# GpSimd's small steps in order of their inputs, three norms of one unit on VectorE, and the filter's turns and weight loads ordered otherwise around it

## The chip, the cores and the metric

The kernel runs on one core of one Trainium2 chip. The metric is the device time of one execution in microseconds (us). All times below are in us unless ns is said.

A core's engines each work off their own instruction stream, and wait for each other at semaphores: TensorE (PE; PEld is its weight load), VectorE (DVE), ScalarE (ACT), GpSimd (POOL) and SyncE (SP), which here only issues DMAs. A DMA that SyncE or GpSimd issues stands in that engine's queue (SPq, POOLq), and runs beside the engines.

## The reference, cut to what matters

Two layers, each a gated long convolution and a GeGLU MLP, over S = 2048 tokens of D = 576 channels, with a hidden size F = 4608. Both layers use the same weights and the same k, v.

```python
def A(q, k, v, shift_k, ssm_k, ssm_D):          # q is the normed x
    k_shift = sum over t < 4 of k_pad[:, t:t+S] * shift_k[:, 3-t]
    kv = k_shift * v
    y = irfft(rfft(kv, 2S) * rfft(ssm_k, 2S))[:S]  # causal convolution along the tokens
    y = y + kv * ssm_D
    return q * y

def B(x):
    return (gelu(x @ w_gate) * (x @ w_up)) @ w_down

x = A_q
x = x + A(layernorm(x), k, v, ...)
x = x + B(layernorm(x))
x = x + A(layernorm(x), k, v, ...)
x = x + B(layernorm(x))
```

The convolution's result y does not depend on x, so both layers use one y; x enters A only through the norm that gates it.

## The kernel before, in words

**Units and passes.** The 2048 tokens are four chunks of 512, a chunk is four pieces of 128 tokens. A unit is one chunk in one layer. There are eight: unit 0 is (layer 0, chunk 0), 1 is (0,1), 2 is (1,0), 3 is (1,1), 4 is (0,2), 5 is (0,3), 6 is (1,2), 7 is (1,3). The passes are [0], [1,2], [3,4], [5,6], [7]: the MLP's weights are streamed through SBUF once in each pass, and the units of a pass share them. A pass has three phases (a third of the hidden size each), and in each phase each of its units has one visit: a gate/up stage of 12 hidden tiles (L1555, `gu`; ScalarE's gelu at L1559, VectorE's product at L1560), then a down stage of four accumulations, one for each piece (L1575, `dn`), which VectorE adds into the residual `x_c` (L1611, or L1606 with the row sum where a layer ends; L1597 into a result tile `ob` where layer 1 ends). TensorE's PSUM comes as tiles of one ring with the tag "pr".

**Weights.** Gate and up weights come in groups of four hidden tiles, `load_wgu(n)`: three DMAs on SyncE (L1137 to L1139). Three such buffers exist, and nine groups make a pass, so groups 9 to 17 serve units 1 and 2, 18 to 26 units 3 and 4, 27 to 35 units 5 and 6, 36 to 44 unit 7. Down weights are `load_wd` (L1147). Loads wait in the list `due` with a due time; `weights()` issues them at once, unless a unit's input is being made (`near`) and the load is due more than HOLD = 14 later.

**The conv work between.** The convolution is done as an FFT by matmuls, and its small steps fill gaps: `conv.V` (VectorE), `conv.L` (loads and turns), `conv.Pq` (TensorE), `conv.spills` and `conv.late` (GpSimd's DMAs). The filter's `turn(b)` puts a chunk of the filter (`hb`, L419) through four DMA transposes on SyncE, and stores it to `Td` on GpSimd; `filt(b)` loads it back in another order (`hT`, L438, GpSimd), multiplies it by the FFT matrices, and spills the results to `Hd` (L399, GpSimd).

**A unit's input.** `prep(ui, j)` gates piece j on VectorE with y (`mul`, then `add`, L1224, which also sums the row). Then comes a chain of small steps, handed from engine to engine: `mean_after` (GpSimd, `nm`, L1175), `square_task` (ScalarE, `junk`, L1183), `root` (GpSimd, `ve` L1190, `rstd` L1191, `nb` L1195), `norm` (ScalarE, `xn`, L1246, two activations, one of 576 columns and one of the first 64 columns again), and `spread` (SyncE, two DMA transposes into `xnT`, L1265). The next gate/up stage multiplies `xnT`. Where layer 0 ends, a piece of a unit in layer 1 is gated with the same chain in front of it: its mean, squares and root come from the down stage's result.

**What sets the order.** The instruction order is written by a small planner at build time. It keeps an estimated clock for TensorE, VectorE and ScalarE (`t.pe`, `t.dve`, `t.act`) with fixed costs (`C_*`). Between the matmul groups it calls `fill`, which issues due weights, loads and turns, transposes of finished pieces (`spreads`), VectorE's tasks (`run_vq` from the queue `vq`, and `conv.run_v`), at most one ScalarE task (`run_aq`: first the norms in `nq`, then the squares in `aq`), and GpSimd's steps (`conv.flush`). GpSimd's small steps (the means and roots) and its DMAs stand in one queue, `spills`, first in, first out: a step goes when the one at the head is due. A small step is due AHEAD = 3.0 before its input is expected:

```python
        conv.spills.append((when - AHEAD, run))
...
    def flush(self, now, keep=0):
        while len(self.spills) > keep and self.spills[0][0] <= now:
            self.spills.popleft()[1]()
```

At run time each engine goes through its instructions in that order and waits where an input or a buffer is not there yet.

Of the kernel before, what the change touches and what calls it, by code (L numbers as in the profile page):

```python
# [16 lines left out]
ALU = mybir.AluOpType  # L17
# [16 lines left out]
C_GU, C_DN = 1.944, 0.245  # L34
C_PR = 1.25
C_BF, C_TB, C_R4 = 0.41, 0.46, 0.77
C_SQ, C_TINY, C_NA, C_ROOT, C_NB = 0.85, 0.6, 0.95, 1.5, 0.4
N_KC, N_SM, N_EO, N_HR = 4, 4, 4, 3
C_AC, C_AB = 0.76, 0.76
C_TT, C_ST, C_HT, C_GELU, C_EVA, C_EVD = 0.76, 0.82, 0.69, 0.6, 0.66, 0.76  # L40
LAG = 0.25
AHEAD, CHAINED = 3.0, 2.5
LATE = (1, 2)
HOLD, LEAD, HURRY, SPARE = 14.0, 1.8, 2.6, 4.0

# [39 lines left out]
class Conv:  # L85
# [9 lines left out]
    def __init__(self, spare, tc, ctx, pace, A_k, A_v, A_shift_k, A_ssm_k, A_ssm_D, ident, psp, cpsp, ypool):  # L95
        self.tc, self.nc, self.t = tc, tc.nc, pace
        self.spare = spare
        self.k2, self.v2, self.hk = A_k[0], A_v[0], A_ssm_k
        self.S, self.D = self.k2.shape
        self.NB = self.S // BS  # L100
        self.KS = A_shift_k.shape[1]
        self.sk, self.sD = A_shift_k, A_ssm_D
        self.ident, self.psp, self.cpsp, self.ypool = ident, psp, cpsp, ypool
        D = self.D
        pool = lambda name, bufs: ctx.enter_context(tc.tile_pool(name=name, bufs=bufs))
        self.cst = pool("c_cst", 1)
        self.krp = pool("c_kr", 3)
        self.hrp = pool("c_hr", N_HR)
        self.kcp = pool("c_kc", N_KC)
        self.ybp = pool("c_yb", 4 * RT)  # L110
        self.prp = pool("c_pr", 3)
        self.smp = pool("c_sm", N_SM)
        self.eop = pool("c_eo", N_EO)
        self.kvp = pool("c_kv", 1)
        self.Hd = [[tc.dram_tile([P, 2 * D], BF16, name=f"Hd{b}_{t}") for t in range(RT)] for b in range(self.NB)]
        self.Kd = [[tc.dram_tile([P, 2 * D], BF16, name=f"Kd{b}_{t}") for t in range(RT)] for b in range(self.NB - 1)]
        self.W = self.cst.tile([P, 24, P], BF16, name="W")
        self.Td = [None, None] + [tc.dram_tile([BS, D], BF16, name=f"Td{b}") for b in range(2, self.NB)]
        self.skc = self.cst.tile([P, self.KS, D], BF16, name="skc")
        self.y, self.yb = {}, {}  # L120
        self.kt_, self.vt_ = {}, {}
        self.y_at = {(0, j): 0.0 for j in range(RT)}
        self.kv_at, self.fwd_at, self.filt_at, self.td_at, self.hd_at = {}, {}, {}, {}, {}
        self.turn_at = 0.0
        self.y_used = {}
        self.startup, self.other = True, False
        self.h1_at = {2: 0.0}
        self.z_at, self.then = {}, []
        self.load_at, self.tight = -9.0, lambda: False
        self.nps = 0  # L130
        self.ps_free = self.spare_free = self.last = 0.0
        self.window = -1.0
        self.pr_free = [0.0] * N_SM
        self.neo, self.eo_free = 0, [0.0] * N_EO
        self.U = deque()
        self.kr_free, self.hr_free = [0.0] * 3, [0.0] * N_HR
        self.npr = self.nkr = self.nhr = 0
        self.V, self.L, self.Pq = deque(), deque(), deque()
        self.left = 0
        self.spills, self.late = deque(), deque()  # L140

    def halves(self, ap):
        return ap.rearrange("p (h c) -> p h c", h=2)
# [259 lines left out]
    def store(self, dst, t, ready):  # L403
        self.spills.append((ready, lambda: self.nc.gpsimd.dma_start(out=dst, in_=t[:])))  # L404

    def flush(self, now, keep=0):
        while len(self.spills) > keep and self.spills[0][0] <= now:
            self.spills.popleft()[1]()

    def turn(self, b):  # L410

        nc, t, D = self.nc, self.t, self.D
        own = {}

        def piece(i):
            def run():
                if i == 0:
                    own["t"] = self.kvp.tile([P, RT, D], BF16, tag="k", name="hb")
                nc.sync.dma_start_transpose(out=own["t"][:, i:i + 1, :],  # L419
                                            in_=self.hk[:, b * BS + i * P:b * BS + (i + 1) * P])  # L420
                self.turn_at = t.pe + 3.5
                if i == RT - 1:
                    def out():
                        nc.gpsimd.dma_start(out=self.Td[b].rearrange("(t p) d -> p t d", p=P), in_=own["t"][:])
                        self.td_at[b] = t.pe + 9.0
                    self.late.append((t.pe + 14.0, out))
            return run
        for i in range(RT):
            self.L.append((lambda i=i: max(self.turn_at, self.kv_at.get(1, NEVER) if b == 2 else self.td_at.get(b - 1, NEVER)),
                           piece(i)))  # L430

    def filt(self, b):
        nc, t, D = self.nc, self.t, self.D
        kc, own = {}, {}

        def load():
            own["t"] = self.kvp.tile([P, RT, D], BF16, tag="v", name="hT")
            nc.gpsimd.dma_start(out=own["t"][:], in_=self.Td[b].rearrange("(p i) d -> p i d", i=RT))  # L438
            own["at"] = t.pe + 9.0
        self.L.append((lambda: max(self.fwd_at.get(b - 1, NEVER), self.td_at.get(b, NEVER)), load))  # L440

        def out():
            if not kc:
                self.flush(NEVER)
                kc.update({k: self.kcp.tile([P, 2, D], BF16, tag="kc", name="hc") for k in range(RT)})
            return kc

        def seen(h):
            if h == 1:
                self.filt_at[b] = t.pe + 0.25  # L450

        def done(kt, h, when):
            if h == 1:
                for k in (kt, kt + 2):
                    self.spill(self.Hd[b][k], kc[k], when, (b, k))
        for h in range(2):
            self.Pq.extend(self.quarter(lambda: own["t"], out, h, lambda: max(own.get("at", NEVER), self.z_at[b - 1]()), seen, done))
            self.Pq.extend(self.then)
            self.then = []

    def step(self, m, kv=None, loaded=False):
# [65 lines left out]

        def out4():
            if not kc:
                self.flush(NEVER)  # L530
                kc.update({k: self.kcp.tile([P, 2, D], BF16, tag="kc", name="kc") for k in KTS})
            return kc

# [31 lines left out]
        def add(kt, a, part):  # L565
            def run():
                slot, pr = prs[(kt, a, part)]
                second = a == seq(kt)[1]
                if second:
                    if quad and kt % 2:  # L570
                        self.flush(NEVER)
                        f = self.kcp.tile([P, 2, HW], F32, tag="kc", name="zs")
                    else:
                        f, zslot[(kt, part)] = self.eo_tile("zs")
# [505 lines left out]
def ssm_geglu_kernel(ctx, tc, A_q, A_k, A_v, A_shift_k, A_ssm_k, A_ssm_D, B_x, B_w_gate, B_w_up,  # L1080
# [91 lines left out]
    def mean_after(v, when):  # L1172
        def run():
            v["nm"] = small.tile([P, 1], F32, tag=v["pfx"] + "nm", name="nm")
            nc.gpsimd.tensor_scalar(out=v["nm"][:], in0=v["s"][:], scalar1=-1.0 / D, scalar2=None, op0=ALU.mult)  # L1175
            v["nm_at"] = max(t.pe, when) + C_TINY
        conv.spills.append((when - AHEAD, run))

    def square_task(get_x, v):
        def run():  # L1180
# [6 lines left out]
            def root():  # L1187
# [5 lines left out]
                if "norm" in v:  # L1193
# [1 line left out]
                    nc.gpsimd.tensor_tensor(out=v["nb"][:], in0=v["nm"][:], in1=v["rstd"][:], op=ALU.mult)  # L1195
                    ready = v["rstd_at"] + C_NB
                    nq.append((lambda: NEVER if len(xn_made) >= 3 else ready, C_NA, lambda: v["norm"](ready)))
            conv.spills.append((when - AHEAD, root))
        aq.append((at_v(v, "nm_at"), C_SQ, run))

    def run_aq(limit):
        for q in (nq, aq):
            if q and q[0][0]() <= t.pe + 1.4 and max(t.act, t.pe - 1.0) + q[0][1] <= limit:
                q.popleft()[2]()
                return

    def gate2_steps(c, j, g, v, second):
        src = lambda: (x_c if second else x_b)[c][:, j, :]
# [30 lines left out]
    def prep(ui, j):  # L1239
# [2 lines left out]

        def norm(ready):
            xn = xnp.tile([P, XW], BF16, tag="xn", name="xn")
            for lo, hi, c0 in ((0, D, 0), (D, XW, 0)):
                nc.scalar.activation(out=xn[:, lo:hi], in_=x_c[c][:, j, c0:c0 + hi - lo], func=ACT.Identity,  # L1246
                                     scale=v["rstd"][:, 0:1], bias=v["nb"][:, 0:1])
            xn_made.append((ui, j, xn, t.on_act(C_NA, max(ready, t.pe - 1.0)) + 0.3))
        v["norm"] = norm
        return gate2_steps(c, j, (hvars if layer else gvars)[c][j], v, layer == 1)  # L1250

    hvars = {}

# [44 lines left out]
    def spreads():  # L1298
        while xn_made and xn_made[0][3] <= t.pe:
            ui, j, xn, _ = xn_made.popleft()  # L1300
            if j == 0:
                xnT_of[ui] = xtp.tile([P, NKC, CH], BF16, tag="xnT", name="xnT")
            spread(xnT_of[ui], j, xn)
            xn_done[ui] = j + 1

    due = []

# [4 lines left out]
    def weights():  # L1312

        while due:
            near = xn_made or nq
            if near and due[0][0] > t.pe + HOLD:
                break
            _, _, load, n = due.pop(0)
# [7 lines left out]
    def fill(limit, tensor, conv_first):  # L1326
# [3 lines left out]
        while True:  # L1330
# [3 lines left out]
            else:  # L1334
                done = run_vq(limit)
                if done is None or not (done or conv.run_v(limit)):
                    break
        run_aq(min(limit, t.pe + 2.3))
        conv.flush(t.pe)
        if tensor and (hurry() or t.pe > conv.last + (CHAINED if chained() else 0.0)):  # L1340
            for _ in range(3):
# [3 lines left out]
    with tc.manual_schedule():  # L1345
# [36 lines left out]
        def act_sum0(j):  # L1382
            sum_task(0, j, gvars[0][j])
            aq.pop()[2]()
            conv.spills.pop()[1]()

        def act_sq0(j):
            square_task(lambda: x_b[0][:, j, :], gvars[0][j])
            aq.pop()[2]()
            conv.spills.pop()[1]()  # L1390

        xn0 = {}

# [19 lines left out]
        def sq0(j):  # L1413
            square_task(lambda: x_c[0][:, j, :], vs0[j])
            aq.pop()[2]()
            roots[j] = conv.spills.pop()[1]

        def std0(j):
            v = vs0[j]
# [85 lines left out]
                return kind[1:] >= LATE  # L1505
            return kind is not None and need[0] == "y2" and need[1:3] not in conv.y_at
        now = lambda: wanted() or hurry() and (t.pe > 60.0 or conv.fresh > 0)
        conv.tight = chained
        visits = []
        for pi, us in enumerate(passes):  # L1510
            visits += [(pi * NP + ph, ph, ui, k == 0, k == len(us) - 1)
# [154 lines left out]
```

## Time and profile before

| what | value |
|---|---|
| time of the runs, median of 3 | 919.99 (919.54 to 920.04) |
| the profiled execution's own time | 919.67 |
| its span in the trace | 917.5 |
| instructions | 19275 |
| busy: TensorE, VectorE, ScalarE, GpSimd | 99%, 63%, 35%, 17% of the span |
| VectorE's product `hT` (L1560) | x276, 686 ns each |
| ScalarE's gelu (L1559) | x276, 596 ns each |
| ScalarE's `xn` (L1246), both shapes | x56, mean 644 ns |
| GpSimd's `nm`, `ve`, `rstd` | 346, 343, 662 ns |
| SyncE's queue (q1) | 93.47 MB, 48.5% of the 16 DMA engines' span |
| GpSimd's queue (q0) | 36.43 MB, 12.2% |

The page is of one execution, whose span runs from its first to its last instruction; its time, 919.67, holds 2.2 outside the span. A line of a timeline gives the start, the duration, the engine, the line of the kernel, the operation, and out<-in with shapes; "xN" is a run of N like instructions, and the bracket at the end is the idle time ahead of it and what ended that. A line on DMAs gives the queue, the count, the size and the time from issue to landing.

### The profile page before, as it was taken

Reading aid. Unit: us, or ns where it says so; the run is one execution under the profiler, and the core shown is the slowest. Engines: PE = TensorE matmul, PEld = TensorE weight load, DVE = VectorE, ACT = ScalarE, POOL = GpSimd, SP = SyncE. Lnnn points to the kernel's source line nnn. Section 1 sums busy time; section 2 is a strip of 40 time slices with the busy share of each in tenths; the row PEclk is TensorE's granted clock in tenths of the full one; section 3 lists DMA queues with packets and bytes.
Section 4 is the critical chain, followed back from the end, with each engine's and each line's share of the span. In section 5 each row is a group of like instructions: output and inputs, shape, how many; then the busy total and the mean of one; then the engine's idle time right before and its main releaser. Section 6 shows DMA issues by size and latency. Waiting matters only on the chain.

```text
span 917.5 us, 19275 instructions
## 1 busy us (share of the span) xinstructions
PE 908.0 (99%) x8198; PEld 530.3 (58%) x8198; DVE 575.2 (63%) x976; ACT 325.1 (35%) x608; POOL 156.8 (17%) x337
## 2 busy tenths in 40 slices
PE   8999999999999999999999999999999999999998
PEld 6786555465565564654655655646646546556555
DVE  7988976479889886685698897443333335322332
ACT  6843256633224135452224124551121224321211
POOL 3512024210115032150013202220000003100000
PEclk9999999999999999999999999999999999999999
DMA  9998988929528618776734900980720821697720
GB/s 256 325 257 252 197 179 145 270 81 223 169 79 190 192 14 135 190 152 153 178 100 100 253 24 30 164 170 19 138 79 2 155 79 27 117 220 172 138 66 26
DMA packets 128954, 131.14 MB, mean 143 GB/s; under 512 B 43618, under 2 KB 120675, under 8 KB 128868
## 3 DMA queue, kind: packets, MB, share of 16 engines
q1 hardware_dynamic: 119232, 93.47, 48.5%
q0 software_dynamic: 9632, 36.43, 12.2%
q8 instruction: 64, 1.05, 0.5%
q14 instruction: 22, 0.18, 0.1%
q10 hardware_dynamic: 4, 0.01, 0.0%
HBM read 108.35 MB, written 11.80 MB: 131 GB/s over the span
## 4 chain that ended last, share of the span: by engine, by line
PE 91%; issue 3%; DVE 2%; ACT 1%; DMA 1%; POOL 1%; SPq 0%; ACTq 0%; DVEq 0%; POOLq 0%
PE gu L1555 55%; PE dn L1575 28%; PE gu L1480 3%; DMA out_dram<-ob 1%; PE ps L214 1%; PE cps L389 1%; PE cps L289 1%; POOL rstd L1191 0%; ACT junk L1183 0%; PE ps L389 0%; DVE wx L926 0%; DVE x_c L1224 0%; PE ps L289 0%; SPq L1265 0%; PE cps L214 0%
## 5 line engine op out<-in xcount | busy, mean ns | idle before, releaser
L1555 PE MATMUL gu<-xnT,wgu 64*128 64x512 bf16 x4968 | 541.4, 377 | 2.4 <-DMA xnT<-xn 1.5
L1555 PEld LDWEIGHTS <-wgu 64*128 64x128 bf16 x4968 | 241.9, 94 | 295.0 <-issue 7.6
L1559 ACT ACTIVATE ga<-gu 128x512 f32<-128x512 f32 x276 | 164.6, 596 | 484.6 <-PE gu L1555 475.3
L1560 DVE TENSOR_TENSOR hT<-ga,gu 128x512 bf16<-128x512 f32 x276 | 189.3, 686 | 213.6 <-ACT ga L1559 211.4
L1575 PE MATMUL dn<-wd,hT 128*128 128x288 bf16 x2304 | 292.2, 287 | 0.0
L1575 PEld LDWEIGHTS <-hT 128*128 128x128 bf16 x2304 | 223.3, 98 | 65.7 <-issue 9.7
L1611 DVE TENSOR_TENSOR x_c<-x_c,dn 128x576 f32<-128x576 f32 x64 | 48.1, 752 | 57.5 <-PE dn L1575 57.5
L1175 POOL TENSOR_SCALAR nm<-s 128x1 f32<-128x1 f32 x60 | 20.7, 346 | 287.9 <-DVE x_c L1606 203.8
L1183 ACT ACTIVATE junk<-x_c,nm 128x576 bf16<-128x576 f32 x48 | 36.9, 768 | 24.2 <-POOL nm L1175 22.8
L1191 POOL TENSOR_TENSOR rstd<-ve,neghalf_t 128x1 f32<-128x1 f32 x62 | 41.0, 662 | 5.2
L519 POOL DMA_DIRECT2D hr<-Hd x32 | 17.5, 547 | 114.9 <-DVE prod L348 114.0
L1246 ACT ACTIVATE xn<-x_c,nb,rstd 128x576 bf16<-128x576 f32 (+1 forms) x56 | 33.3, 644 | 10.1 <-POOL nb L1195 10.1
L1597 DVE TENSOR_TENSOR ob<-x_c,dn 128x576 bf16<-128x576 f32 x15 | 11.3, 754 | 27.4 <-PE dn L1575 15.3
L1190 POOL TENSOR_SCALAR ve<-ss 128x1 f32<-128x1 f32 x62 | 21.3, 343 | 38.5 <-ACT junk L1183 38.3
L1480 PE MATMUL gu<-xnT,wgu 64*128 64x256 bf16 x432 | 24.6, 270 | 0.0
L292 ACT COPY eo<-cps 128x576 f32<-128x576 f32 x26 | 16.5, 636 | 18.6 <-PE cps L289 13.9
L349 DVE TENSOR_TENSOR prod<-prod 128x576 bf16<-128x576 bf16 x48 | 22.0, 458 | 1.7
L1480 PEld LDWEIGHTS <-wgu 64*128 64x128 bf16 x432 | 20.8, 94 | 3.3 <-issue 0.7
L404 POOL DMA_DIRECT2D out_dram<-ob x12 | 6.7, 557 | 85.8 <-DVE ob L1597 65.8
L252 DVE SCALAR_TENSOR_TENSOR eo<-eo 128x576 f32<-128x576 f32 x20 | 14.8, 753 | 5.7 <-ACT eo L292 5.7
L577 DVE TENSOR_TENSOR zs<-sum,prod 128x576 f32<-128x576 bf16 x24 | 18.1, 754 | 0.3
L580 DVE TENSOR_TENSOR zs<-zs,prod 128x576 f32<-128x576 f32 x24 | 18.1, 753 | 0.2
(166 smaller groups left out, 551.7 us busy)
## 6 DMA issues: line engine op xcount, KB each, us to landing
wgu<-in_B_w_gate_dram SPq DMA_DIRECT2D x45, 576.0 KB, 5.8
wd<-in_B_w_down_dram SPq DMA_DIRECT2D x30, 864.0 KB, 7.1
wgu<-in_B_w_up_dram SPq DMA_DIRECT2D x45, 512.0 KB, 7.8
hr<-Hd POOLq DMA_DIRECT2D x32, 288.0 KB, 5.4
kr<-Kd POOLq DMA_DIRECT2D x24, 288.0 KB, 5.2
Kd<-kc POOLq DMA_DIRECT2D x12, 288.0 KB, 5.2
k<-in_A_k_dram POOLq DMA_DIRECT2D x3, 1008.0 KB, 11.6
wgu<-in_B_w_up_dram SPq DMA_DIRECT2D x45, 64.0 KB, 8.0
```

Of the source, the lines that this page charges most:

```text
L349: nc.vector.tensor_tensor(out=dst, in0=pr[:, 0, :], in1=pr[:, 1, :], op=ALU.subtract if part == 0 else ALU.add)
L1175: nc.gpsimd.tensor_scalar(out=v["nm"][:], in0=v["s"][:], scalar1=-1.0 / D, scalar2=None, op0=ALU.mult)
L1183: nc.scalar.activation(out=junk[:], in_=get_x(), func=ACT.Square, bias=v["nm"][:, 0:1], accum_out=v["ss"][:])
L1190: nc.gpsimd.tensor_scalar(out=ve[:], in0=v["ss"][:], scalar1=1.0 / D, scalar2=EPS, op0=ALU.mult, op1=ALU.add)
L1191: nc.gpsimd.tensor_tensor(out=v["rstd"][:], in0=ve[:], in1=neghalf_t[:, 0:1], op=ALU.pow)
L1246: nc.scalar.activation(out=xn[:, lo:hi], in_=x_c[c][:, j, c0:c0 + hi - lo], func=ACT.Identity, scale=v["rstd"][:, 0:1], bias=v["nb"][:, 0:1])
L1480: nc.tensor.matmul(pair[:, s, e * 256:(e + 1) * 256], lhsT=w[r0:r0 + HK, k, gi * P:(gi + 1) * P], rhs=xnT[r0:r0 + HK, blk_of[k], tok], sta ...
L1555: nc.tensor.matmul(pair[:, s, :], lhsT=w[r0:r0 + HK, k, gi * P:(gi + 1) * P], rhs=xnT[r0:r0 + HK, b, :], start=(k == 0), stop=(k == NKC - 1))
L1559: nc.scalar.activation(out=ga[:], in_=pair[:, 0, :], func=ACT.Gelu_apprx_tanh)
L1560: nc.vector.tensor_tensor(out=hT[:, fi, :], in0=ga[:], in1=pair[:, 1, :], op=ALU.mult)
L1575: nc.tensor.matmul(part[h][:, h, 0:HW], lhsT=hT[:, fi, at * P:(at + 1) * P], rhs=wd[2 * wb + fi // WT][:, fi % WT, h * HW:(h + 1) * HW], s ...
L1611: nc.vector.tensor_tensor(out=xh, in0=xh, in1=acc[:, :, 0:HW], op=ALU.add)
```

## The change

- **GpSimd's order.** Means and roots leave the first-in-first-out queue: `small_step` keeps them in a list of their own, and `flush` takes from it whichever is due first, ahead of the DMAs. Where the filter's or the FFT's stores are flushed to free buffers, small steps no longer go with them. They are due 2.0 before their input instead of 3.0.
- **Norms of unit 1.** Pieces 0, 2 and 3 are normed on VectorE (`norm_v`: one `tensor_scalar` and a copy of 64 columns), without `nb` on GpSimd; piece 0's is queued behind the gate steps of piece 1, the other two behind those of piece 3. Piece 1 stays on ScalarE. All other units stay on ScalarE.
- **ScalarE's queue.** `run_aq` is called until it finds nothing more to issue, instead of once.
- **Turns of the filter** are held while a normed piece waits for its transposes or a norm is queued.
- **Weight loads** are held for a unit's input only until all four pieces of unit 1 have been handed to SyncE; from then on they are issued when their turn in `due` comes.

```diff
-AHEAD, CHAINED = 3.0, 2.5
+AHEAD, CHAINED = 2.0, 2.5
...
-    def flush(self, now, keep=0):
+    def small_step(self, ready, run):
+        self.nstep += 1
+        self.steps.append((ready, self.nstep, run))
+
+    def flush(self, now, keep=0, steps=True):
+        while steps and self.steps:
+            first = min(self.steps)
+            if first[0] > now:
+                break
+            self.steps.remove(first)
+            first[2]()
         while len(self.spills) > keep and self.spills[0][0] <= now:
             self.spills.popleft()[1]()
...
-            self.L.append((lambda i=i: max(self.turn_at, self.kv_at.get(1, NEVER) if b == 2 else self.td_at.get(b - 1, NEVER)),
+            self.L.append((lambda i=i: max(self.turn_at, NEVER if self.turning() else 0.0, self.kv_at.get(1, NEVER) if b == 2 else self.td_at.get(b - 1, NEVER)),
                            piece(i)))
...
             if not kc:
-                self.flush(NEVER)
+                self.flush(NEVER, steps=False)
...
-        conv.spills.append((when - AHEAD, run))
+        conv.small_step(when - AHEAD, run)
...
-            conv.spills.append((when - AHEAD, root))
+            conv.small_step(when - AHEAD, root)
...
                 q.popleft()[2]()
-                return
+                return True
+        return False
...
-        v["norm"] = norm
-        return gate2_steps(c, j, (hvars if layer else gvars)[c][j], v, layer == 1)
+
+        def norm_v(j):
+            def run():
+                v = nvars[ui][j]
+                xn = xnp.tile([P, XW], BF16, tag="xn", name="xn")
+                nc.vector.tensor_scalar(out=xn[:, 0:D], in0=x_c[c][:, j, :], scalar1=v["nm"][:, 0:1],
+                                        scalar2=v["rstd"][:, 0:1], op0=ALU.add, op1=ALU.mult)
+                nc.vector.tensor_copy(out=xn[:, D:XW], in_=xn[:, 0:HK])
+                xn_made.append((ui, j, xn, t.dve + C_NV + 0.3))
+            return ("v", nvars[ui][j], "rstd_at"), C_NV, run
+        tasks = gate2_steps(c, j, (hvars if layer else gvars)[c][j], v, layer == 1)
+        if ui > 1 or j == 1:
+            v["norm"] = norm
+        if ui == 1:
+            tasks += [norm_v(i) for i in {1: (0,), 3: (2, 3)}.get(j, ())]
+        return tasks
...
-            near = xn_made or nq
+            near = (xn_made or nq) and xn_done.get(1, 0) < RT
...
-        run_aq(min(limit, t.pe + 2.3))
+        while run_aq(min(limit, t.pe + 2.3)):
+            pass
...
-        conv.tight = chained
+        conv.tight, conv.turning = chained, lambda: bool(xn_made or nq)
```

More of the change, by code (lines that the diff above doesn't have):

```diff
@@ L36 @@
 C_BF, C_TB, C_R4 = 0.41, 0.46, 0.77
-C_SQ, C_TINY, C_NA, C_ROOT, C_NB = 0.85, 0.6, 0.95, 1.5, 0.4
+C_SQ, C_TINY, C_NA, C_NV, C_ROOT, C_NB = 0.85, 0.6, 0.95, 0.74, 1.5, 0.4
 N_KC, N_SM, N_EO, N_HR = 4, 4, 4, 3
@@ L128, in __init__ @@
         self.z_at, self.then = {}, []
-        self.load_at, self.tight = -9.0, lambda: False
+        self.load_at, self.tight, self.turning = -9.0, lambda: False, lambda: False
         self.nps = 0
@@ L139, in __init__ @@
         self.left = 0
-        self.spills, self.late = deque(), deque()
+        self.spills, self.late, self.steps, self.nstep = deque(), deque(), [], 0
     def halves(self, ap):
@@ L529, in out4 @@
             if not kc:
-                self.flush(NEVER)
+                self.flush(NEVER, steps=False)
                 kc.update({k: self.kcp.tile([P, 2, D], BF16, tag="kc", name="kc") for k in KTS})
@@ L570, in run @@
                     if quad and kt % 2:
-                        self.flush(NEVER)
+                        self.flush(NEVER, steps=False)
                         f = self.kcp.tile([P, 2, HW], F32, tag="kc", name="zs")
@@ L1244, in norm @@
             xn = xnp.tile([P, XW], BF16, tag="xn", name="xn")
-            for lo, hi, c0 in ((0, D, 0), (D, XW, 0)):
-                nc.scalar.activation(out=xn[:, lo:hi], in_=x_c[c][:, j, c0:c0 + hi - lo], func=ACT.Identity,
+            for lo, hi in ((0, D), (D, XW)):
+                nc.scalar.activation(out=xn[:, lo:hi], in_=x_c[c][:, j, 0:hi - lo], func=ACT.Identity,
                                      scale=v["rstd"][:, 0:1], bias=v["nb"][:, 0:1])
             xn_made.append((ui, j, xn, t.on_act(C_NA, max(ready, t.pe - 1.0)) + 0.3))
-        v["norm"] = norm
-        return gate2_steps(c, j, (hvars if layer else gvars)[c][j], v, layer == 1)
+        def norm_v(j):
[13 more added lines that the diff above has]
+        return tasks
     hvars = {}
@@ L1300, in spreads @@
             ui, j, xn, _ = xn_made.popleft()
-            if j == 0:
+            if ui not in xnT_of:
                 xnT_of[ui] = xtp.tile([P, NKC, CH], BF16, tag="xnT", name="xnT")
             spread(xnT_of[ui], j, xn)
-            xn_done[ui] = j + 1
+            xn_done[ui] = xn_done.get(ui, 0) + 1
     due = []
@@ L1384, in act_sum0 @@
             aq.pop()[2]()
-            conv.spills.pop()[1]()
+            conv.steps.pop()[2]()
         def act_sq0(j):
@@ L1389, in act_sq0 @@
             aq.pop()[2]()
-            conv.spills.pop()[1]()
+            conv.steps.pop()[2]()
         xn0 = {}
@@ L1415, in sq0 @@
             aq.pop()[2]()
-            roots[j] = conv.spills.pop()[1]
+            roots[j] = conv.steps.pop()[2]
         def std0(j):
```

## The prediction

> **What bounds the kernel now.** I read the page first: the chip runs at the full clock in every slice, and TensorE is busy for nearly the whole span.
>
> ```profile
> span 917.5 us, 19275 instructions
> PE 908.0 (99%) x8198; PEld 530.3 (58%) x8198; DVE 575.2 (63%) x976; ACT 325.1 (35%) x608; POOL 156.8 (17%) x337
> ```
>
> The order of the two kernels' instructions, laid side by side, is the same for all 16398 TensorE rows. So the change can only move the places where TensorE waits. I looked for those in TensorE's own timeline: behind the start-up (which is unchanged) there are two, at 159 and at 810.
>
> ```profile
> 159.09 0.39 PE L1555 MATMUL gu<-xnT,wgu 64*128 64x512 bf16 x2 [0.75 <-DMA xnT<-xn]
> 160.21 2.12 PE L1555 MATMUL gu<-xnT,wgu 64*128 64x512 bf16 x18 [0.73 <-DMA xnT<-xn]
> ...
> 807.23 2.12 PE L1555 MATMUL gu<-xnT,wgu 64*128 64x512 bf16 x18
> 809.88 2.12 PE L1555 MATMUL gu<-xnT,wgu 64*128 64x512 bf16 x18 [0.53 <-DVE ob L1597]
> 812.36 19.60 PE L1555 MATMUL gu<-xnT,wgu 64*128 64x512 bf16 x180 [0.36 <-DVE ob L1597]
> ```
>
> An undisturbed gate/up stage takes 23.42 from its start to that of the next down stage (82.94 to 106.36). The stage of unit 1 should start at 158.27, when the down stage before it ends, and the next starts at 183.41 instead of 181.69: **1.73 lost** to the last transposes of unit 1's input. The stage of unit 7 takes 831.89 - 807.23 = 24.66: **1.24 lost** to VectorE's result tile, which waits for a store. A third, smaller place shows only in the sums: the down stage at 402.95 takes 13.22 to 416.17, the one at 439.59 with the same eight filter matmuls 12.85: **0.37 lost**. The change can win at most 1.73 + 1.24 + 0.37 = 3.3.
>
> **What stands behind the stall at 159.** SyncE's queue, in time:
>
> ```profile
> 146.28 2.55 SPq L1265 DMA_TRANSPOSE xnT<-xn  x2
> 148.87 1.26 SPq L419 DMA_TRANSPOSE hb<-in_A_ssm_k_dram  x1
> 150.66 8.25 SPq L1265 DMA_TRANSPOSE xnT<-xn  x6
> 159.01 0.63 SPq L1137 DMA_DIRECT2D wgu<-in_B_w_gate_dram  x1
> ```
>
> Each transpose costs SyncE about 1.26; a filter turn stands between pieces 0 and 1; the last transpose is issued at 157.65 and lands 2.5 later, at 160.17. In the changed order the filter's last turn goes behind piece 3, but weight group 11 (three loads) and one filter turn go between pieces 1 and 2. What that does to landing shows where before has it so, at 577 to 580, in the answers on DMAs for two short windows (issue to landing):
>
> ```profile
> xnT<-xn SPq DMA_TRANSPOSE x2, 2.5
> ...
> wgu<-in_B_w_up_dram SPq DMA_DIRECT2D x1, 64.0 KB, 7.2
> xnT<-xn SPq DMA_TRANSPOSE x1, 7.0
> ```
>
> Ahead of a weight group a transpose lands after 2.5, right behind one after 7.0, just after the weights: the queue's transfers come out in order.
>
> **Unit 1, step by step.** *GpSimd's order.* Before, root 0 (L1190) stood behind the mean of piece 1, which waits for VectorE: squares done at 139.66, `ve` at 141.56. Now it comes right after the squares: `rstd` by 139.75 + 0.27 + 0.56 = 140.6. *VectorE.* Three norms are added, each 0.58 + 0.18 by the start-up's rows of the same form (L1357, L1359). Norm 0 falls at 142.7 to 143.5; the gate step behind it slides by 0.76, and 0.79 of idle time ahead of the product at 145.21 takes that up. Norms 2 and 3 stand behind the accumulation of down piece 0 (149.56 to 150.32), and end at 151.1 and 151.9. VectorE then holds the accumulations of down pieces 1 up to 1.1 longer; TensorE needs that PSUM slot only at 158.3, so this is free by 4. *ScalarE* loses three pairs of 1.19 and keeps norm 1 where the first norm was, 145.07 to 146.26. *GpSimd* loses three `nb` of 0.19.
>
> *SyncE.* Piece 0 goes at 143.6, piece 1 at 146.3 to 148.8. Weight group 11 needs the buffer that gate/up frees at 146.48, so its issue starts at 148.9. Groups 9, 10, 18 and 27 had moved all their data about 7.45 after their first issue (126.20 to 133.5, for one), so it is through at 156.35. The filter turn is issued at 150.95, pieces 2 and 3 from 152.25 to 157.4, all before that. Behind group 27 the first two transposes took 1.35 more and the next two 1.2; the filter turn is half a piece. That makes 1.35 + 1.2 + 0.6 = 3.15, data through at 159.5, landed near 159.8. TensorE resumes 0.4 before 160.21: **-0.4**, not -1.73. The issue is 1.5 earlier (156.15), but the queue gives 1.1 of it back. From below, without the weights in front, the last transpose would land at 158.65 and win 1.5; from above see the first rival. I take the queue, since four weight groups agree.
>
> **Unit 4's turn (0.37).** Before, roots 2 and 3 waited behind the filter's stores:
>
> ```profile
> 395.70 1.29 POOL L399 DMA_DIRECT2D Hd<-hc  x2 [3.75 <-DVE hc L265]
> 397.01 0.44 POOL L1190 TENSOR_SCALAR ve<-ss 128x1 f32<-128x1 f32 x1
> 397.54 0.97 POOL L1191 TENSOR_TENSOR rstd<-ve,neghalf_t 128x1 f32<-128x1 f32 x1
> ...
> 403.24 1.20 ACT L1246 ACTIVATE xn<-x_c,nb,rstd 128x576 bf16<-128x576 f32 x2 [1.53 <-POOL nb L1195]
> 404.34 0.57 ACT L1559 ACTIVATE ga<-gu 128x512 f32<-128x512 f32 x1
> 404.82 0.62 ACT L292 COPY eo<-cps 128x576 f32<-128x576 f32 x1
> ```
>
> Their squares had ended at 394.7 and 396.6. Now the roots go first and both norms go one gelu earlier on ScalarE, the last at 399.73, so nothing is ahead of the copy at 404.82 but a gelu at 403.1. **-0.37** (from both sides: 0 if another wait comes up there, and not more than the 0.37 lost). The four stores slide behind root 3, by 2 to them, and are early for the loads at 403. The last transpose of unit 4 had landed at 416.26, just as its stage began; it now goes to the queue about 3.5 earlier.
>
> **Unit 7's stall (1.24).** Before, SyncE held groups 36, 37, 38 behind all of unit 7's transposes and issued them from 791.27 to 801.2; the first result store, issued at 800.81, took 8.1 to land, and VectorE's third result waited 6.86 for it. The changed order puts group 36 behind piece 1, 37 behind piece 2, 38 behind piece 3. Their buffers come free at 779.75, 787.5 and 795.4, so only 38 is in the queue at 800 and is through by 795.4 + 7.45 = 802.9. The store then lands by about 805; the third result is due at 804.3 and TensorE wants it by 809. **-1.24**, bounded by 0 and 1.24. Unit 7's last piece now lands behind group 37, near 797, ten ahead of 807.
>
> **The other moved steps, at nothing.** Unit 3: its last piece stands behind group 19 (356.2 + 7.45 + 1.2, some 365), needed at 379.5. Unit 5: its last piece behind group 29 (buffer free at 583.65, data at 591.1, transposes at 592.5), needed at 595.53: cover 3.0. Chunk 3's filter store on GpSimd goes from 167.4 to about 171, the `k` load behind it lands some 4 later than 182.2; VectorE reads it at 193.0. The loop around ScalarE's queue and the smaller lead of 2.0 change no other order.
>
> **Sum.** -1.24 - 0.37 - 0.4 = -2.0 against the profiled execution's 919.67, that is 917.7. The median of the runs is 919.99, 0.32 above it; so 918.0. A measurement tells about 0.2%, 1.84, from no change.
>
> **Rival 1, slower: the filter's load runs into the last transposes.** GpSimd's load `hT` (L438) was issued at 151.62. The transpose issued at 152.35 took 4.8 to land instead of 2.5, and no transpose's data moved between 153.25 and 155.25, the time in which `hT` did. In the changed order `hT` stands behind the root of unit 2's gate piece 1: accumulation 153.6 to 154.4, mean 154.7, squares to 155.9, root to 156.9, issue at 157.0, its data from 158.65 if the start takes 1.65 again. If that is ahead of the last transposes' end at 159.5, they wait out the 2.65 of its data and land near 162.2: the seam loses 2.0 more instead of winning 0.4, and the sum is +0.4, 920.4. The price rises to +2.3 (922.3) if piece 2 is caught as well. For it: the two times are within 1. Against: with weights in front, GpSimd's transfers started later (store 800.81: 6; `x_b` 160.41: 5). It decides if `hT` data starts before 159.5. [...]
>
> [...] The trace has GpSimd's steps at 0.44, 0.97 and 0.81 at 397 to 399 against 0.19, 0.57 and 0.19 at 144.7. Were the norms to do that, two roots ahead of `hT` would move it by some 2.5, to data at 161, past the transposes; the sum stays.
>
> **Rival 2: the store still lands late** behind group 38 (8.1 as before): the 1.24 stays, 919.2. **Rival 3: weights and transposes overlap after all**, all three stalls go: 919.99 - 3.3 = 916.7; the 7.0 speaks against it. **Rival 4: unit 5's last piece is late**, after a queue as slow as 10.2 (group 11 before: 159.01 to 169.21): 595.1, barely inside, so it needs more: slower by 2.
>
> **Chances.** Forecast 0.46 (0.41 over 0.2% faster, 0.05 within); rival 1 0.32 (half within, half slower, where piece 2 is caught as well); rival 2 0.06 within; rival 3 0.09 faster; rival 4 0.07 slower. Faster 0.50, same 0.27, slower 0.23. Range 916.7 to 922.0, from rival 3 to nearly the whole of rival 1; the forecast alone 917.5 to 918.5.
>
> **What would show it.** In the profile after: unit 1's second gate/up matmul pair near 159.8 (162 by rival 1), its last transpose with an issue near 156.1 and over 3 to landing; the stage from 807 taking 23.42 with no wait for `ob`; the down stage at 403 taking 12.85. The forecast is wrong if any TensorE wait stands elsewhere, at 595 above all.

## The result, and the profile after

The change makes the kernel slower: median 923.42 (922.59 to 924.01, 5 runs) against 919.77 (919.21 to 920.04, 5 runs), ratio 1.0041, 95% interval 1.0026 to 1.0055. That is outside the forecast range, on the slow side. The profiled execution took 923.42 with a span of 921.5, 4.0 more than before.

The page of the changed kernel: the span, TensorE's busy time, and the granted clock in 40 slices.

```profile
span 921.5 us, 19273 instructions
PE 909.2 (99%) x8198; PEld 530.6 (58%) x8198; DVE 577.1 (63%) x982; ACT 322.1 (35%) x602; POOL 160.8 (17%) x334
...
PEclk9999999899999999999999999999999999999999
```

One digit of the clock's row is an 8, in the slice from 161 to 184. TensorE's timeline, from the end of unit 0's last visit on, has one wait left, and it stands there:

```profile
163.43 25.62 PE L1581 MATMUL gu<-xnT,wgu 64*128 64x512 bf16 x216 [5.06 <-DMA xnT<-xn]
188.98 0.42 PE L1601 MATMUL dn<-wd,hT 128*128 128x288 bf16 x2
...
408.52 0.42 PE L1601 MATMUL dn<-wd,hT 128*128 128x288 bf16 x2
...
421.36 3.85 PE L1581 MATMUL gu<-xnT,wgu 64*128 64x512 bf16 x34
...
812.42 23.48 PE L1581 MATMUL gu<-xnT,wgu 64*128 64x512 bf16 x216
835.84 0.42 PE L1601 MATMUL dn<-wd,hT 128*128 128x288 bf16 x2
```

The starts give the whole balance. Unit 1's next down stage starts at 188.98 instead of 183.41: **5.57 lost** at the seam to unit 1. The down stage at 408.52 takes 12.84 to 421.36 instead of 13.22: 0.38 won. Unit 7's gate/up stage takes 23.42 (812.42 to 835.84) instead of 24.66: 1.24 won. 5.57 - 0.38 - 1.24 = 3.95, the difference of the spans.

The seam, first in SyncE's timeline:

```profile
143.51 5.96 SPq L1290 DMA_TRANSPOSE xnT<-xn  x4
149.58 0.64 SPq L1147 DMA_DIRECT2D wgu<-in_B_w_gate_dram  x1
150.26 1.02 SPq L1148 DMA_DIRECT2D wgu<-in_B_w_up_dram  x1
151.33 0.63 SPq L1149 DMA_DIRECT2D wgu<-in_B_w_up_dram  x1
152.01 1.27 SPq L429 DMA_TRANSPOSE hb<-in_A_ssm_k_dram  x1
153.37 6.47 SPq L1290 DMA_TRANSPOSE xnT<-xn  x4
```

The last four transposes took 6.47 to issue instead of four times 1.26: the second took 2.57, and the last was issued at 158.57. GpSimd's load of the filter, `hT` (not VectorE's product of the same name), went out at 157.59:

```profile
157.59 0.63 POOL L448 DMA_DIRECT2D hT<-Td  x1
```

The answer on DMAs for 159.6 to 161.6 shows who had the engines (q0 is GpSimd's queue, q1 SyncE's):

```profile
q0 software_dynamic: 95, 0.44, 96.4%
q1 hardware_dynamic: 38, 0.01, 1.9%
```

For these two microseconds the transposes all but stood still behind `hT`. The last ones landed at 163.29 and 163.65.

The clock, in windows of 3.42 laid where the granted clock changed (us, TensorE busy and count, clock, DMA share, GB/s):

```profile
157.54:160.96 3.42, 0.82 (x7) 1.00 1.15 207
160.96:164.38 3.42, 0.95 (x6) 0.50 1.39 264
164.38:167.80 3.42, 3.42 (x20) 0.50 0.80 242
167.80:171.20 3.40, 3.40 (x36) 1.00 1.09 358
```

From 160.96 to 167.80 TensorE was granted half its clock, though it was fully busy in the second half of that. So the stage took 25.62 instead of 23.48. The loss at the seam, 7.3 against 1.7 before, is 5.1 of waiting and 2.1 of half clock (25.55 from the stage's start to that of the next, instead of 23.42).

### The profile page after: what moved, and what is told of

Same layout as the page of the kernel before. It is cut to its first block, busy times and chain, and to the rows that moved or that the text cites. A ratio compares the mean times of both kernels' runs of the same rounds, so it can differ in the third digit from the quotient of the medians.

```text
span 921.5 us, 19273 instructions
## 1 busy us (share of the span) xinstructions
PE 909.2 (99%) x8198; PEld 530.6 (58%) x8198; DVE 577.1 (63%) x982; ACT 322.1 (35%) x602; POOL 160.8 (17%) x334
## 4 chain that ended last, share of the span: by engine, by line
PE 96%; DVE 1%; ACT 1%; DMA 1%; POOL 0%; issue 0%; ACTq 0%; POOLq 0%; DVEq 0%
PE gu L1581 59%; PE dn L1601 30%; PE gu L1506 3%; PE ps L214 1%; PE cps L389 1%; PE cps L289 1%; DMA xnT<-xn 1%; PE ps L389 0%; PE ps L289 0%; DVE wx L936 0%; PE cps L214 0%; ACT junk L1193 0%; PE cps L873 0%; DVE wx L939 0%; POOL rstd L1201 0%
## 5 line engine op out<-in xcount | busy, mean ns | idle before, releaser
L1200 POOL TENSOR_SCALAR ve<-ss 128x1 f32<-128x1 f32 x62 | 24.5, 395 | 56.0 <-ACT junk L1193 55.8
L1257 ACT ACTIVATE xn<-x_c,nb,rstd 128x576 bf16<-128x576 f32 (+1 forms) x50 | 29.8, 644 | 6.0 <-POOL nb L1205 5.9
L1235 DVE SCALAR_TENSOR_TENSOR x_c<-g_t,rstd,x_c 128x576 f32<-128x576 f32 x16 | 13.0, 814 | 9.2 <-POOL rstd L1201 9.2
```

What stands on the lines that cost most here:

```text
L1200: nc.gpsimd.tensor_scalar(out=ve[:], in0=v["ss"][:], scalar1=1.0 / D, scalar2=EPS, op0=ALU.mult, op1=ALU.add)
L1257: nc.scalar.activation(out=xn[:, lo:hi], in_=x_c[c][:, j, 0:hi - lo], func=ACT.Identity, scale=v["rstd"][:, 0:1], bias=v["nb"][:, 0:1])
```

## The experiments

Times are medians against runs of the kernel before on the same chip (919.4 to 919.8).

**Who makes the transposes late.** Three runs move two DMAs of the changed kernel and nothing else.

```diff
 e1: the filter's load hT later
-            self.L.append((lambda: max(..., self.td_at.get(b, NEVER)), load))
+            self.L.append((lambda: max(..., self.td_at.get(b, NEVER), self.parted.get(1, NEVER) + 3.0), load))
 (parted[1] is the planned time at which unit 1's last piece goes to SyncE)
 e2: weight group 11 behind pieces 2 and 3, in weights()
+            if 0 < xn_done.get(1, 0) < RT:
+                break
 e3: both
```

> The changed kernel with one DMA moved: the filter's load hT on GpSimd's queue is held until 3.0 planned us after unit 1's last piece has gone to SyncE. In the issue order it stands four small steps later; it should be issued near 160.4 instead of 157.59. Nothing else moves. The changed kernel lost 5.06 at the seam to unit 1 (158.36 to 163.43), and the stage behind it took 25.62 instead of 23.42. Theory A (weight group 11, ahead of pieces 2 and 3 in SyncE's queue, pushes the last transposes into hT's data; both are needed): with hT gone the transposes that stood still from 159.5 to 161.5 go on, the last ones land near 161.2, the stall is about 2.9, the clock stays up or falls for less, and the time comes to between 919.0 and 921.2. Theory B (hT alone costs it): the seam is at 159.8 or better, 916.5 to 917.5. Theory C (weight group and late norms alone; hT costs nothing): 923.4, unchanged.

> The changed kernel with one thing moved: weight group 11's three loads stand behind the transposes of unit 1's pieces 2 and 3 in SyncE's queue instead of ahead of them; hT stays where it is (issue 157.59, data from 159.5). Theory A: the last transposes are issued near 155 and land by 158.7, before hT's data, so the stall is at most 0.7 and the clock stays: 923.4 - 4.4 - 2.2 = 916.8. Theory B (hT alone costs the stall, wherever the weights are): hT's data still meets the last transposes, and the time stays over 920. Theory C: as theory A, 916.8. A later group 11 (issue near 156.3, landing within 10 of it) is needed at 174, so it costs nothing.

> The changed kernel with both moved: hT as in the first of these runs, weight group 11 as in the second. Theory A: no better than with group 11 moved alone, 916.8 within 0.5, since the transposes are through before hT starts either way. Theory B: 916.8 here and with hT moved alone, over 920 with group 11 moved alone. Theory C: 916.8 here and with group 11 moved alone.

Measured: with `hT` later 920.32 (918.36 to 921.97; ratio 1.0005, 0.9996 to 1.0015), with group 11 later **915.72** (915.66 to 916.08; 0.9956, 0.9941 to 0.9971), with both later 916.13 (0.9959, 0.9944 to 0.9974). TensorE's timeline with `hT` later, then with group 11 later:

```profile
160.55 0.39 PE L1584 MATMUL gu<-xnT,wgu 64*128 64x512 bf16 x2 [2.36 <-DMA xnT<-xn]
161.59 24.90 PE L1584 MATMUL gu<-xnT,wgu 64*128 64x512 bf16 x214 [0.65 <-DMA xnT<-xn]
```

```profile
158.14 23.48 PE L1583 MATMUL gu<-xnT,wgu 64*128 64x512 bf16 x216
```

That is theory A. (The two runs with the group later came in below the forecast of 916.8, the first by 1.1, since nothing is left of a stall that was allowed up to 0.7.) Moving `hT` alone is worth 2 in waiting, and `hT` does harm only because group 11 has made the transposes late: with the group behind them they are all issued by 156.48, no wait at all is left, and `hT` at its old place costs nothing. Theories B and C fall. The version with group 11 later beats the kernel before by 0.44%; its span is 914.0, 3.5 less, and all three of the old stalls are gone.

**What lowers the clock.** The changed kernel with extra matmuls in the stall, on weights that are there already and into a PSUM tile that is overwritten:

```diff
+                if wb == NP and ui == 1 and fi == 0:
+                    for _ in range(22):      # 8 and 16 in the other two runs
+                        for s, r0 in ((0, 0), (1, HK)):
+                            nc.tensor.matmul(pair[:, s, :], lhsT=w[r0:r0 + HK, 0, 0:P], rhs=w[r0:r0 + HK, 0, :], start=True, stop=True)
```

> The changed kernel with 44 extra matmuls on TensorE (22 pairs of 64x128x512 on weights that are already there, into the PSUM tile that the first gate/up tile then overwrites) between unit 0's last down stage and unit 1's first gate/up stage: 22 x 0.217 = 4.8 us of work in a stall of 5.06. They change nothing in what is waited for. Theory 1 (the granted clock falls to 0.50 because TensorE stood idle for 5 us): the stall is filled, the clock stays at 1.00, the stage takes 23.42 instead of 25.62, and the time falls by 2.2 to 921.2. Theory 2 (the clock falls for another cause, as the load of the DMA engines or a fixed moment): the stage still takes 25.6 and the time is 923.4 or a little more.

> The changed kernel with 16 of the extra matmuls (8 pairs) instead of 44 in the stall: 1.8 us of work, so TensorE stands idle for some 3.3 instead of 5.06. The stall's end does not move. If the clock's fall hangs on the length of the idle time with a limit between 1.0 (no loss in the run with the stall filled) and 2.4 (a loss of 1.6 in the run with hT later), it falls here too, and the time is 922.6 to 923.4; if the limit lies above 3.3, or the loss grows in proportion, 921.2 to 922.4.

> The changed kernel with 32 of the extra matmuls (16 pairs) in the stall: 3.5 us of work, so TensorE stands idle for some 1.5 instead of 5.06. With 2.95 idle the time was of two kinds, 921.2 and 922.7. If the clock's fall needs an idle time over some 2, it stays up in all runs here: 921.2. If its chance falls in proportion, some runs are near 922.7.

Measured: 22 pairs 921.17 (920.98 to 922.66), 16 pairs 921.18 (921.04 to 921.69), 8 pairs 922.68 (921.16 to 922.92). More work on TensorE, and 2.2 less time: theory 1. TensorE's timeline with 22 pairs:

```profile
158.25 4.92 PE L1581 MATMUL gu<-wgu 64*128 64x512 bf16 x44
164.16 23.62 PE L1585 MATMUL gu<-xnT,wgu 64*128 64x512 bf16 x216 [0.99 <-DMA xnT<-xn]
```

This is the slowest of its ten executions, 922.66, and its stage starts 0.7 later than without the filling; but it takes 23.62, and the clock stays full. With 8 pairs, 2.95 idle in the profile, there are two kinds of runs, four from 922.63 to 922.92 with a mean clock of 0.998, and two of 921.16 and 921.19 with 1.000. The run with `hT` later has three kinds: 918.36 and 919.25 at 1.000, seven from 919.91 to 920.96 at 0.998, one of 921.97 at 0.996. The steps fit one and two stretches of half clock: the changed kernel's profile, at 0.996, has two of 3.42, and the profiled execution of this run, at 0.998, has one, between the windows

```profile
158.10:161.52 3.42, 0.48 (x3) 1.00 0.94 181
161.52:164.94 3.42, 3.35 (x16) 0.50 0.94 226
164.94:168.36 3.42, 3.42 (x34) 1.00 1.11 210
```

The stretch of half clock is 3.42 long here, and 6.84, twice that, in the changed kernel. The 3.42 ahead of a fall were not wholly idle: TensorE was busy for 14% of them here (0.48 of 3.42) and for 24% in the changed kernel (0.82).

With 8 pairs the window ahead of the fall was 31% busy (1.07 of 3.42, from 160.72 to 164.14). In the kernel before, a window that was 57% busy (1.93 of 3.41, from 158.03 to 161.44) was followed by no fall; and with 1.61 of waiting, in the next run below, no window of 3.41 can have been less than 53% busy (1.80), and the clock of its profiled execution stayed at 1.00. So if the busy share of such a window decides, which is my reading, the limit lies somewhere between 31% and 53%, as far as one execution of each can tell. The falls fit a fixed grid in the traces' record of the clock, where the half-clock stretch of the changed kernel is 6.827 long, two of 3.413: the clock fell 150.19 after its first rise in the changed kernel and with `hT` later, which is 44 times 3.413, and 153.60 after it with 8 pairs, which is 45 times. On such a grid an idle time of 3 falls into one window or is shared by two. That would give the two kinds of runs, but it is not shown: of these two kernels only runs at 0.998 were profiled.

**How SyncE's issue is held up.** The run with `hT` later, and the filter's turn 3.2 behind piece 3 as well:

```diff
-  max(self.turn_at, NEVER if self.turning() else 0.0, ...
+  max(self.turn_at, NEVER if self.turning() or b == 3 and i > 1 and 1 not in self.parted else 0.0, ...
```

> The run with hT later, with the filter turn 3.2 also moved: from between weight group 11 and piece 2 to behind piece 3 in SyncE's queue (3.3 follows it one turn later). With hT later, the second transpose of piece 2 was the third behind the group; its issue took 2.92 instead of 1.26, until the group's data was through, and the last transpose was issued at 159.05 and landed at 161.55. Theory A (SyncE's issue of the third transpose behind a weight group is held up until the group's data is through; what lands last is set by the issues after that): one transpose fewer behind the group brings the last issue 1.3 forward, to about 157.7, and its landing to 160.2; the stall shrinks from 3.0 to about 1.7, the clock stays up, 917.5 to 918.3. Theory D (only the data in the queue counts): half a piece of data, 0.6 earlier, landing near 161, a stall of 2.4, 918.5 to 920.

Measured: 917.71 (917.53 to 920.31; ratio 0.9983, 0.9973 to 0.9992). SyncE's timeline of this run:

```profile
151.84 6.57 SPq L1291 DMA_TRANSPOSE xnT<-xn  x4
158.45 1.27 SPq L430 DMA_TRANSPOSE hb<-in_A_ssm_k_dram  x1
```

Again one of the four was held, now the first of piece 3 (2.60), the third transpose behind the group. The last was issued at 157.14 and landed at 159.77, 1.78 earlier than the 161.55 with the turn ahead; TensorE waited 1.61. That is theory A, with a little more than it asked, of which 0.33 is that group 11 itself went out earlier here (148.90 against 149.23); half a piece of data less would have given 0.6. What exactly holds the third, these runs do not show.

**One part of the change at a time.** Each is made on the kernel before, the last on the changed one.

```diff
 f1: the weight rule alone
-            near = xn_made or nq
+            near = (xn_made or nq) and xn_done.get(1, 0) < RT
 f2: small_step, flush with steps, AHEAD 2.0, and nothing else of the change
 g2: norm_v for pieces 0, 2 and 3 of unit 1, and nothing else of the change
 f3: the changed kernel with all norms on ScalarE
-        if ui > 1 or j == 1:
-            v["norm"] = norm
-        if ui == 1:
-            tasks += [norm_v(i) for i in {1: (0,), 3: (2, 3)}.get(j, ())]
+        v["norm"] = norm
```

> The kernel before with one line of the change: weight loads are held for a unit's input only until unit 1's four pieces have gone to SyncE. This moves groups 19, 27, 28, 29, 36, 37 and 38 ahead of pieces in SyncE's queue, and nothing on any other engine. If the prediction's step holds, unit 7's stage (24.66 before) takes 23.42, no result tile waits for its store, and the rest stays: 1.24 less, 918.4 to 918.6. The rival (another part of the change took the store's wait away, or unit 5's last piece comes too late behind group 29): no gain, or a wait of TensorE near 595.

> The kernel before with GpSimd's small steps taken in order of their inputs (the list of its own, ahead of the stores, due 2.0 ahead), the norms all on ScalarE, turns and weight loads by the old rules. If the prediction's step holds, the down stage before unit 4's unit turn (13.22 before) takes 12.85, unit 7's stage still takes 24.66, and unit 1's seam keeps most of its 1.73, because filter turns still stand between its pieces and the last transpose is issued by SyncE as before: 919.2 to 919.8. The rival (the first-in-first-out order was what held up unit 1): the seam's 1.73 goes too, 917.6.

> The kernel before with one part of the change: unit 1's norms of pieces 0, 2 and 3 on VectorE; GpSimd's order, turns and the weight rule are the old ones. These norms wait in VectorE's queue, which the weight rule does not look at, so group 11 goes between pieces 1 and 2 with no other change. If that is what costs: the last transpose lands near 161 or later, the stall at the seam is 2.5 to 5, with a fall of the clock for part of the runs, and the time 920.5 to 925; unit 7 and unit 4 keep their losses. If the cost needs the other parts too (the new order of GpSimd puts hT in the way): the seam is as before or better, 919.0 to 920.0.

> The changed kernel with unit 1's norms back on ScalarE. A norm then waits in the list that the weight rule looks at, so group 11 is held until all four pieces are handed over, with no other rule added; the filter's turns 3.2 and 3.3 go behind too, and with them hT's use on TensorE comes later. If the three VectorE norms matter only by hiding the pieces from the weight rule: the seam's stall is under 0.8, the clock stays, the other gains (1.24 and 0.37) stay, 916.0 to 917.0. If they matter by their speed: the last piece lands after 160 as before, 917.4 or more. If the later filter steps cost: TensorE waits elsewhere, 918 or more.

| run | median | ratio (95%) | lost at the seam | unit 4 | unit 7 |
|---|---|---|---|---|---|
| before | 919.4 to 919.8 | | 1.71 | 13.22 | 24.66 |
| weight rule alone | 918.19 | 0.9985 (0.9975 to 0.9995) | 1.34 | 13.22 | 23.41 |
| small steps alone | 918.01 | 0.9984 (0.9975 to 0.9993) | 1.04 | 12.85 | 24.43 |
| VectorE norms alone | 924.06 | 1.0047 (1.0032 to 1.0062) | 6.0 | 13.23 | 24.43 |
| changed, norms on ScalarE | 918.73 | 0.9991 (0.9982 to 1.0001) | 1.6 | 12.84 | 23.42 |

"Lost at the seam" is the start of the down stage behind unit 1's first visit, less the start of the one ahead of it, less 35.29 (11.87 and 23.42); the other columns are the stages' times. The weight rule and the small steps do what the prediction said of them. Both runs are below what was expected of them, the first by 0.2, the second by 1.2: the small steps also win 0.7 at the seam, where the last transpose lands at 159.49 instead of 160.17 (the weight rule, which moves nothing ahead of this seam, shows 0.4 there, so some of it may be a run's own scatter), and 0.2 in unit 7's stage (24.43), which the run with the norms alone shows as well. The three norms alone cost 4.4: group 11 goes between pieces 1 and 2 with no other part of the change. TensorE's timeline of that run:

```profile
162.41 25.07 PE L1568 MATMUL gu<-xnT,wgu 64*128 64x512 bf16 x216 [4.33 <-DMA xnT<-xn]
```

`hT` is in the way here too: issued at 152.87, it had 88.0% of the DMA engines' time from 158.3 to 159.5, between the group and the transposes. So the 6.0 is not the group's alone.

The root is in the planner: `weights()` asks whether a piece waits in `xn_made` or `nq`. A norm on ScalarE stands in `nq`; a norm on VectorE stands in `vq`, where the rule does not look, and between pieces 1 and 2 the rule sees nothing near. The norms themselves are good: with the group held, the seam loses nothing with them on VectorE (158.14 above), and 1.6 with them on ScalarE, where the norms of pieces 1 to 3 ran from 148.88 to 152.25 and the last transpose was issued at 157.33 instead of 155.22. That last run is 3.0 slower than 915.72; half of it is the seam, and the rest comes in stages where its filter work stands elsewhere, which I did not take apart.

## Why the prediction was wrong, step by step

- **The orders and the engines' part: right.** Norm 0 on VectorE ran from 142.70 (forecast 142.7), norms 2 and 3 ended at 151.05 and 151.75 (151.1, 151.9), piece 0 went to SyncE at 143.51 (143.6), piece 1 at 146.30.
- **Unit 4 (-0.37) and unit 7 (-1.24): right to 0.01.** The first result store was issued at 806.00 and landed in 3.7 instead of 8.1. The runs of single parts put these gains where the prediction put them, on the small steps and on the weight rule.
- **Unit 1's seam (-0.4): wrong, +5.57.** Three terms failed. The first is the order in SyncE's queue, "pieces 2 and 3 from 152.25 to 157.4": group 11 and the turn came 1.1 later than planned (its second load took 1.02 to issue, and its start was 149.58), and then the third transpose behind the group was held to 157.21, so that the last was issued at 158.57 and not 156.15. The prediction took 1.26 for each issue, so that all were through before the group's data, and then added up data alone (1.35 + 1.2 + 0.6). In fact the last issue decided: with `hT` out of the way it came at 159.05, and landing 2.5 later, at 161.55, not 159.8. The row was in the profile of before: behind group 27, four transposes took 6.87.

```profile
580.01 6.87 SPq L1265 DMA_TRANSPOSE xnT<-xn  x4
```

- **The second failed term is the weighing of rival 1.** The prediction gave `hT` an issue at 157.0 and data from 158.65, and took the transposes to be through by 159.5. `hT` was issued at 157.59 with data from 159.5, but the transposes were later by more. Its argument against ("with weights in front, GpSimd's transfers started later") was true by 0.3, and not enough. It is rival 1's case; its "2.65 of its data", which stands in no row, is the two microseconds above, in which `hT` took 96.4% of the engines' time. A slowing of GpSimd's steps by the norms, priced at 2.5, was small: the two steps beside the norms took 0.42 and 0.48 (142.90, 150.44) instead of 0.19 and 0.22; that the norms are the cause was not shown.
- **The third is a cost that no row of before shows: the clock.** Rival 1's landing near 162.2 would already have been 4 of idle time, and the prediction priced it as waiting only. The runs with the stall filled show 2.2 for it.
- **Rival 2 and rival 3** fall: the store was early, and transposes did not pass weights (the one issued at 154.64, behind group 11, landed after 5.1 instead of 2.5). **Rival 4** was closer than thought: unit 5's last piece landed at 600.23, 0.5 ahead of its stage at 600.72 where the prediction had a cover of 3.0. There too the third transpose behind a group (28) was held 3.17, which put group 29 and the piece behind it later. In one profiled run with the stall filled, TensorE waited 0.21 there.

## What to carry to other kernels

When work is moved to another queue, look for every rule that reads the old queue to decide something else: the three norms won 1.6 at their seam, and the load that slipped in ahead of their transposes cost 7.7 (923.42 against 915.72). A DMA ahead of a critical one in the same queue must be priced with the issue that it holds up (four transposes took 6.47 here, where four times 1.26 is 5.04), not with its data alone, and by the row of the same kind in the profile of before. A stall on TensorE cost its length here, and when it was long one or two stretches of 3.42 at half clock as well: in all five runs with 5.06 of idle time in the profile, in 8 of 10 with 3.01, in 4 of 6 with 2.95. With 1.61 it was one run of ten, with 1.06 none of ten. (Two runs of the kernel before, 921.54 and 921.58, have a mean clock of 0.998 too; no profile shows where they lost it.)

## What the runs showed of the hardware that was not expected

- The granted clock fell to 0.50 behind idle times of 2.95 and 3.01, less than one of its stretches of 3.42, and 44 needless matmuls in the stall made the changed kernel 2.2 faster.
- A transfer of 576 KB from GpSimd's queue left SyncE's transposes 1.9% of the DMA engines' time for two microseconds, while it took 96.4%; it moves packets of 4608 bytes, they move packets of 256.
- SyncE's third transpose behind a weight group took 2.57 to 3.61 to issue instead of 1.26 (154.64 and 586.34 in the changed kernel, 582.75 before, 162.00 with group 11 later). Loads are held up too: of the nine weight loads in a row from 791.27 before, the last two took 2.75 and 2.34 to issue instead of 0.63.
